# One fused attention-and-MLP kernel: partial products begun in PSUM by copies, weights split two operands at a time, activation differences on DVE, and four batches of attention first

## The chip, the core and the metric

The kernel runs on one core of one Trainium2 chip. Its time is the device time of one execution in microseconds (us): 1303.35 us before the change, the median of 3 runs (1302.53 to 1304.0). Engines: PE multiplies matrices into PSUM, DVE, ACT and POOL work on elements, SP issues the DMAs. Each engine takes its instructions strictly in the order of its own queue, so an instruction that waits holds up all that stand behind it.

## The reference

```python
B, H, S, D = 8, 12, 448, 64          # 3584 tokens, d_model 768, d_ff 2048
scores = q @ k.T / sqrt(D) - log(S)
attn = 1 / (1 + exp(-scores))        # a sigmoid, no softmax
x = heads_joined(attn @ v)           # (3584, 768)
h = x @ w_in                         # (3584, 2048)
g = h * clip(h + 3, 0, 6) / 6
out = g @ w_out                      # (3584, 768)
```

## The kernel before

**Seven products in place of eight.** Both matrix products of the MLP are cut into 2 x 2 blocks and computed with seven block products, `P1, P5, P6, P2, P7, P3, P4` in this order. Operands are sums and differences of blocks, and so are the results. Two batches together are one `n` (0 to 3).

**Each product in three passes.** An fp32 operand is split into a rounded high part and the rest (`split_w`: ACT casts, L263, DVE subtracts, L264), and PE multiplies high by high, high by low and low by high (`passes`). One product of one `j` is so 3 x 3 = 9 matmuls of 128x128 by 128x448.

**Stages.** The order of all work is written out: every step is put on a list by `at(place, ...)`, `place` being a planned time in us (`TS` for half a step of attention, `TU` for one product), and the list is sorted by it. PE, ACT, DVE and POOL keep this order. The DMAs on SP are put in order by the scheduler. `runs` sets the stages: attention for some batches, then the first MLP product for one `n`, and so on: A0 (batches 0, 1, 2), Q0, A1 (3, 4), Q1, A2 (5, 6), Q2, A3 (7), Q3, and at the end B, the second MLP product for all four `n`.

**Attention (A).** A step is one piece of scores for two heads on PE (`scores`), its sigmoid on ACT (L181), and, two steps later, the product with v on PE (`av`). There are 21 steps to a batch, each of two groups of 8 matmul instructions. `take` copies a finished bank out of PSUM (ACT, L209) and adds the second bank (DVE, L210). `t_ops` makes the block differences of x (POOL, L226) and splits them into the tiles `X` for PE (DVE, L217 and L218, 21 pairs per `n`). The `X` tiles of one `n` take the place of those of the `n` before.

**First MLP product (Q).** `quad(n, j)` for eight `j`: seven products, 63 matmuls. P1, P6, P7 and P4 accumulate on one PSUM bank (`za`), P5, P2 and P3 have banks of their own (`zb`). `keep` copies P1 and P5 to SBUF (ACT, L296), `add` forms the block results from PSUM and these copies (DVE, L301), `gate` applies the activation (ACT L314, DVE L315), `diffs` and `last` form the activation differences (POOL, L319 to L329), and SP stores all seven operands of the second product to DRAM. P6 must wait until P1 has been read, P7 until P1+P6 has been read, P4 until P1+P6+P7 has been read.

**Preparing the weights (prep).** The weights arrive as float64. For each of 16 pieces (`which`, `j`) and two halves `u`: ACT's `head` (L95), DVE's `body` and `tail` (L101, L102, L103, L111, L112; the high part in the tile `ab`, the low part in its second half), POOL's sum of both into the tile `wt` (L118), and after both halves four more sums on POOL (L125) and the store to DRAM (L127 one DMA for `which` 0, L130 seven for `which` 1). `wt` and `ab` have one buffer each, `st` (the loaded float64) two. The 8 pieces of `w_in` are prepared in A0 (five) and Q0 (three), those of `w_out` from Q1 on.

**Second MLP product (B).** `block(n)`: 56 units of 9 matmuls, operands loaded from DRAM, split by `split_2`.

## Time and profile before

| what | value |
|---|---|
| median of the runs shown | 1303.35 us |
| the profiled execution, its time | 1308.08 us |
| its span, first to last instruction | 1306.2 us |
| PE, DVE, ACT, POOL busy | 1153.3, 878.1, 649.4, 376.2 us |
| mean granted clock of PE | 0.946 |

The profiled execution took 4.73 us more than the median of the runs, and 1.88 us of its time lie outside its span. Stages overlap a little; the stage borders used below are those at which PE goes from one kind of matmul to the next. A busy share of the whole span says little here, since the stages have different limits: B runs with PE busy throughout, A and Q do not.

### The profile page before, as it was taken

What the parts mean: (1) busy time and instruction counts of PE and PEld (TensorE: products, weight loads), DVE (VectorE), ACT (ScalarE), POOL (GpSimd) and SP (SyncE); (2) the same over time, 40 slices, a digit from 0 to 9 for tenths busy, and PEclk for the clock granted to TensorE, in tenths of its full rate; (3) what the DMA queues carried; (4) which work ended last, traced back from release to release, by engine and by line L of the source; (5) the groups of instructions that cost most, each with busy time, mean ns of one, the idle gap of its engine ahead of it and who ended that gap; (6) DMA issues with size and microseconds to landing.
All of it is one profiled execution on the core that took longest, in us unless ns stands there. A gap on an engine that the chain in (4) does not pass through costs nothing. (4 is left out here: it accounts for less than half of the span.)

```text
span 1306.2 us, 18625 instructions
## 1 busy us (share of the span) xinstructions
PE 1153.3 (88%) x6720; PEld 904.8 (69%) x6720; DVE 878.1 (67%) x1352; ACT 649.4 (50%) x1150; POOL 376.2 (29%) x310
## 2 busy tenths in 40 slices
...
GB/s 248 299 162 192 217 264 229 206 204 136 156 237 212 236 236 218 142 220 213 198 219 192 79 238 245 199 170 266 263 164 159 145 155 155 114 179 187 114 139 59
DMA packets 81452, 250.26 MB, mean 192 GB/s; under 512 B 9040, under 2 KB 57552, under 8 KB 75856
## 3 DMA queue, kind: packets, MB, share of 16 engines
...
q10 hardware_dynamic: 144, 0.07, 0.0%
...
## 5 line engine op out<-in xcount | busy, mean ns | idle before, releaser
L288 PE MATMUL za<-x,w 128*128 128x448 f32 x1152 | 291.6, 407 | 106.2 <-DVE sn_c L301 48.4
L288 PEld LDWEIGHTS za<-x,w 128*128 128x128 f32 x1152 | 240.1, 212 | 146.7 <-issue 57.6
L397 PE MATMUL y<-x,w 128*128 128x448 f32 x1344 | 314.0, 368 | 0.0
L397 PEld LDWEIGHTS y<-x,w 128*128 128x128 f32 x1344 | 252.4, 188 | 25.4
L264 DVE TENSOR_TENSOR w<-raw,w 128x384 fp32r<-128x384 f32 x224 | 185.2, 837 | 43.8 <-ACT w L263 41.7
L181 ACT ACTIVATE a<-sc,bias_s 128x896 f32<-128x896 f32 x168 | 168.3, 1008 | 90.8 <-PE sc L170 45.4
L288 PE MATMUL zb<-x,w 128*128 128x448 f32 x864 | 196.2, 372 | 1.3 <-DVE x L217 1.1
L201 PE MATMUL pv<-a,v 64*64 64x448 f32 x1152 | 168.8, 561 | 28.1 <-DVE xr L210 23.5
L264 DVE TENSOR_TENSOR w<-w,w 128x384 fp32r<-128x384 f32 x224 | 126.4, 564 | 89.0 <-ACT w L263 88.4
L288 PEld LDWEIGHTS zb<-x,w 128*128 128x128 f32 x864 | 167.1, 194 | 17.3 <-DVE x L217 1.5
L263 ACT CAST w<-w 128x384 fp32r<-128x384 f32 x224 | 115.7, 517 | 126.9 <-PE yb L397 122.7
L397 PE MATMUL yb<-x,w 128*128 128x448 f32 x672 | 175.1, 368 | 0.0
L175 PE MATMUL sc<-qk 64*64 64x448 f32 x1152 | 160.7, 554 | 13.1 <-ACT a L181 7.7
L379 DVE TENSOR_TENSOR x<-gr,x 128x448 fp32r<-128x448 f32 x224 | 141.6, 632 | 7.6 <-ACT x L378 7.6
L118 POOL TENSOR_TENSOR wt<-ab 128x384 f32<-128x384 f32 x64 | 70.5, 1122 | 227.5 <-DVE ab L112 214.9
L397 PEld LDWEIGHTS yb<-x,w 128*128 128x128 f32 x672 | 126.2, 188 | 12.7
L378 ACT CAST x<-gr 128x448 fp32r<-128x448 f32 x224 | 127.2, 568 | 7.9 <-DMA gr<-gd 7.9
L263 ACT CAST w<-raw 128x384 fp32r<-128x384 f32 x224 | 110.7, 506 | 32.0 <-DMA raw<-wd 31.8
L201 PEld LDWEIGHTS pv<-a,v 64*64 64x64 f32 x1152 | 59.4, 138 | 92.7 <-issue 51.4
L175 PEld LDWEIGHTS sc<-qk 64*64 64x64 f32 x1152 | 56.3, 138 | 81.1 <-issue 49.4
L319 POOL TENSOR_TENSOR ga<-g,ga 128x448 f32<-128x448 f32 x32 | 42.6, 1332 | 229.5 <-DVE g L315 195.3
L314 ACT ACTIVATE ga<-sn_h,bias 128x448 f32<-128x448 f32 x32 | 21.4, 669 | 155.2 <-DMA gd<-ga 70.2
...
## 6 DMA issues: line engine op xcount, KB each, us to landing
...
```

The lines of the kernel that those rows point to most:

```text
L118: nc.gpsimd.tensor_tensor(out=o, in0=a[:, hs], in1=b[:, hs], op=ALU.add)
L175: nc.tensor.matmul(sc[halves[h], j, :S], k[halves[j], ks], q[halves[j]], start=True, stop=True)
L181: nc.scalar.activation(a, sc[:, :, :S], AF.Sigmoid, bias=bias_s, scale=scale)
L201: nc.tensor.matmul(pv[b, hp][h][halves[j], :S], v[halves[h], j * NC + c], a[halves[h], j], start=c == 0 and not (second and shared), stop= ...
L263: nc.scalar.copy(w[:, 0], src)
L264: nc.vector.tensor_tensor(out=w[:, 1], in0=src, in1=w[:, 0].bitcast(F32), op=ALU.subtract)
L288: nc.tensor.matmul(z[k][:, :S], w[:, wu, c * P : (c + 1) * P], X[n, k, c][:, xu], start=i == 0 and k in (P1, P5, P2, P3), stop=i == 3 * HC ...
L314: nc.scalar.activation(g[o], h, AF.Relu, bias=bias_3, scale=1.0)
L319: nc.gpsimd.tensor_tensor(out=a[:, 1], in0=g["g12"], in1=g["g11"], op=ALU.subtract)
L378: nc.scalar.copy(x[:, 0], src)
L379: nc.vector.tensor_tensor(out=x[:, 1], in0=src, in1=x[:, 0].bitcast(F32), op=ALU.subtract)
L397: nc.tensor.matmul(z[k][e][:, :S], w[:, wu, e * P : (e + 1) * P], x[:, xu], start=u == 0 and i == 0 and k in (P1, P5, P2, P3), stop=u == H ...
```

## The change

- **PSUM.** P2's bank is begun by a copy of P1 (`seed`, ACT) and P3's bank by P1+P6+P5 (`seed2`, DVE), and PE accumulates on top. The additions `h11` and `h12` fall away, and the gate reads the PSUM banks directly. `h22` stays.
- **Splits.** `split_w` splits two operands at once (128x768 in place of 128x384, four calls for seven products), `split_2` two units at once.
- **Differences.** The four activation differences of a quad go from POOL to DVE. `ga` gets a second buffer.
- **prep.** The tile `ab` is gone: `head` writes straight into `wt`, the body works there, the low part lies in the loaded tile `st` (elements 8 bytes apart), and POOL adds both with one instruction of 768. The planned places are closer: 8 pieces of `w_in` in A0, 15.2 apart; `w_out` three in Q0, three in Q1, two in A2.
- **Stages.** `runs` is (0,1,2,3), (4), (5,6), (7). The differences of x are formed in the tiles `xr` themselves (14 buffers), those of n = 1 at the start of A1.

```diff
-TS = 0.82
-TM = 0.2
+TS = 0.78
+TM = 0.207
...
         def head(u):
-            ab[u] = att.tile([P, 2, 2 * W], F32, tag="ab", name=f"ab_{which}_{j}_{u}")
-            nc.scalar.activation(ab[u][:, 0], st[u][:, :, 1].bitcast(F32), AF.Abs, bias=0.0, scale=2.0**-112)
+            if u == 0:
+                wt[0] = att.tile([P, NW + 1, W], F32, tag="wt", name=f"wt_{which}_{j}")
+            nc.scalar.activation(two(u), st[u][:, :, :, 1].bitcast(F32), AF.Abs, bias=0.0, scale=2.0**-112)
...
-            nc.vector.tensor_scalar(out=bi, in0=ai, scalar1=-(2**23), scalar2=None, op0=ALU.bitwise_and)
+            nc.vector.tensor_scalar(out=high, in0=ai, scalar1=-(2**23), scalar2=None, op0=ALU.bitwise_and)
             nc.vector.scalar_tensor_tensor(
-                out=b, in0=low.bitcast(U32), scalar=2.0**-52, in1=b, op0=ALU.mult, op1=ALU.mult
+                out=e, in0=low.bitcast(U32), scalar=2.0**-52, in1=e, op0=ALU.mult, op1=ALU.mult
             )
-            for h in range(2):
-                hs = slice(h * W, (h + 1) * W)
-                o = wt[0][:, ((P1, P2), (P4, NW))[u][h]]
-                nc.gpsimd.tensor_tensor(out=o, in0=a[:, hs], in1=b[:, hs], op=ALU.add)
+            nc.gpsimd.tensor_tensor(out=a, in0=a, in1=e, op=ALU.add)
...
+    pairs = ((P1, P5), (P6, P2), (P7, P3), (P4,))
+    def split_w(keys, src):
+        w = base.tile([P, 2, 2, W], F32R, tag="w", name=f"w_{'_'.join(map(str, keys[0]))}", bufs=4)
+        h, l = w[:, 0, : len(keys)], w[:, 1, : len(keys)]
+        nc.scalar.copy(h, src)
+        nc.vector.tensor_tensor(out=l, in0=src, in1=h.bitcast(F32), op=ALU.subtract)
...
+        def seed():
+            z[P2] = bank(f"zb_{n}_{j}_{P2}", bk[P2])
+            nc.scalar.copy(z[P2][:, :S], z[P1][:, :S])
+        def seed2():
+            z[P3] = bank(f"zb_{n}_{j}_{P3}", bk[P3])
+            nc.vector.tensor_tensor(out=z[P3][:, :S], in0=z[P1][:, :S], in1=sn["e"], op=ALU.add)
...
-            nc.gpsimd.tensor_tensor(out=a[:, 1], in0=g["g12"], in1=g["g11"], op=ALU.subtract)
-            nc.gpsimd.tensor_tensor(out=a[:, 2], in0=g["g22"], in1=a[:, 1], op=ALU.subtract)
+            nc.vector.tensor_tensor(out=a[:, 1], in0=g["g12"], in1=g["g11"], op=ALU.subtract)
+            nc.vector.tensor_tensor(out=a[:, 2], in0=g["g22"], in1=a[:, 1], op=ALU.subtract)
...
-    runs = [(0, 1, 2), (3, 4), (5, 6), (7,)]
+    runs = [(0, 1, 2, 3), (4,), (5, 6), (7,)]
...
+        if n == 1:
+            t_ops(n, range(HC), now + 1.0, 1.25)
...
-        prep(0, j, (14 + 20 * j) if j < 5 else marks[0] + 12.6 * (j - 5), 5)
-        prep(1, j, marks[1] + 5 + 30 * j, 9)
+        prep(0, j, 12 + 15.2 * j, 6)
```

The first place at which instructions move is the start of the second piece of weights in A0. Before, on ACT, its head (`ab_1_0`) waits for its load and for DVE and POOL to be done with the tile `ab`:

```order
L181 ACTIVATE a_2_3_393<-sc_2_3_388,bias_s 128x896 [waits PE_49,Activation_49]
L181 ACTIVATE a_2_4_404<-sc_2_4_399,bias_s 128x896 [waits PE_49,Activation_49]
L95 ACTIVATE ab_1_0_410<-st_1_0_342 128x768 [waits DMAHW7_49,DVE_49,Pool_49]
L181 ACTIVATE a_2_5_420<-sc_2_5_412,bias_s 128x896 [waits PE_49,Activation_49]
L209 COPY xr_2_437<-pv_2_0_378 128x448 [waits PE_49]
```

Before, on POOL, it is the first sum of this piece that also waits for a DMA (`DMAHW3`), the store of the piece before out of the one buffer of `wt`:

```order
L125 TENSOR_TENSOR wt_0_146<-wt_0_146 128x384 [waits Pool_49] x2
L125 TENSOR_TENSOR wt_0_146<-wt_0_146 128x384
L125 TENSOR_TENSOR wt_0_146<-wt_0_146 128x384 [waits Pool_49]
L118 TENSOR_TENSOR wt_1_341<-ab_1_0_410 128x384 [waits DMAHW3_49,DVE_49,Pool_49]
L118 TENSOR_TENSOR wt_1_341<-ab_1_0_410 128x384
```

Now, on ACT, from the second head of the first piece (`wt_0`) to the first head of the second (`wt_1`):

```order
L100 ACTIVATE wt_0_196<-st_0_1_189 128x768 [waits DMAHW3_49]
L180 ACTIVATE a_1_2_265<-sc_1_2_252,bias_s 128x896 [waits PE_49,Activation_49]
L180 ACTIVATE a_1_3_284<-sc_1_3_279,bias_s 128x896 [waits PE_49,Activation_49]
L180 ACTIVATE a_1_4_297<-sc_1_4_292,bias_s 128x896 [waits PE_49,Activation_49]
L180 ACTIVATE a_1_5_308<-sc_1_5_303,bias_s 128x896 [waits PE_49,Activation_49]
L208 COPY xr_1_321<-pv_1_0_267 128x448 [waits PE_49]
L180 ACTIVATE a_1_6_332<-sc_1_6_316,bias_s 128x896 [waits PE_49,Activation_49]
L180 ACTIVATE a_2_0_343<-sc_2_0_338,bias_s 128x896 [waits PE_49,Activation_49]
L100 ACTIVATE wt_1_356<-st_1_0_290 128x2x384 [waits DMAHW7_49,DMAHW3_49,Pool_49]
L180 ACTIVATE a_2_1_358<-sc_2_1_351,bias_s 128x896 [waits PE_49,Activation_49]
```

The head of the second piece now waits for two DMAs, its load (`DMAHW7`) and the store of `wt_0` (`DMAHW3`, on which SP's next load from that place, `raw_0_0<-wd_0`, waits too). All sigmoids behind it wait with it. Between the first heads of two pieces stand 10 sigmoids (9 once).

The second place is the second quad of Q0 on DVE. Before, with a half piece of weights (`ab_6_1`) in it:

```order
L301 TENSOR_TENSOR sn_1_c_1456<-za_1_1381,sn_1_1_1436 128x448
L101 TENSOR_SCALAR ab_6_1_1444<-ab_6_1_1444 128x768
L102 TENSOR_SCALAR ab_6_1_1444<-ab_6_1_1444 128x768
L103 SCALAR_TENSOR_TENSOR ab_6_1_1444<-st_6_1_1312,ab_6_1_1444 128x768
L264 TENSOR_TENSOR w_2_1_1461<-raw_2_0_1269,w_2_1_1461 128x384
L111 TENSOR_SCALAR ab_6_1_1444<-ab_6_1_1444 128x768
L112 SCALAR_TENSOR_TENSOR ab_6_1_1444<-st_6_1_1312,ab_6_1_1444 128x768
L301 TENSOR_TENSOR sn_1_h_1479<-zb_1_3_1446,sn_1_0_1420 128x448
L315 SCALAR_TENSOR_TENSOR ga_1_1481<-ga_1_1481,sn_1_h_1479 128x448
L264 TENSOR_TENSOR w_2_2_1484<-raw_2_0_1269,w_2_2_1484 128x384
L301 TENSOR_TENSOR sn_1_h_1497<-za_1_1381,sn_1_1_1436 128x448
```

Now, from `seed2` (L295) over a half piece (`wt_0`, L106 to L112), a double split (L253) and a gate (L316) to `h22` (L299), on which PE's P4 waits:

```order
L295 TENSOR_TENSOR zb_1_5_1734<-za_1_1668,sne_1_1714 128x448
L106 TENSOR_SCALAR wt_0_1636<-wt_0_1636 128x768
L107 TENSOR_SCALAR wt_0_1636<-wt_0_1636 128x768
L108 SCALAR_TENSOR_TENSOR wt_0_1636<-st_0_1_1648,wt_0_1636 128x768
L111 TENSOR_SCALAR st_0_1_1648<-wt_0_1636 128x768
L112 SCALAR_TENSOR_TENSOR st_0_1_1648<-st_0_1_1648 128x768
L253 TENSOR_TENSOR w_2_2_1753<-raw_2_1_1623,w_2_2_1753 128x768
L316 SCALAR_TENSOR_TENSOR ga_1_1751<-ga_1_1751,zb_1_3_1698 128x448
L299 TENSOR_TENSOR snh_1_1768<-za_1_1668,sne_1_1714 128x448
L316 SCALAR_TENSOR_TENSOR gc_1_1770<-gc_1_1770,snh_1_1768 128x448
```

Four additions of a quad have become two, seven splits four, and the five instructions of a half piece stand between `seed2` and `h22` in one block. The four differences (L320 to L326) follow at the end of the quad on DVE.

More of the change, by code (lines that the diff above doesn't have):

```diff
@@ L252, in tile_kernel @@
-    ring, rawt = {}, {}
-    def load_w1(n, j, part):
-        ks = (slice(0, 4), slice(4, NW))[part]
-        t = one.tile([P, ks.stop - ks.start, W], F32, tag=f"raw{part}", name=f"raw_{n}_{j}_{part}")
-        nc.sync.dma_start(out=t, in_=wd1[j][:, ks])
-        for i, k in enumerate(range(ks.start, ks.stop)):
-            rawt[n, j, k] = t[:, i]
-    def split_w(key, src):
-        w = base.tile([P, 2, W], F32R, tag="w", name=f"w_{'_'.join(map(str, key))}", bufs=8)
-        nc.scalar.copy(w[:, 0], src)
-        nc.vector.tensor_tensor(out=w[:, 1], in0=src, in1=w[:, 0].bitcast(F32), op=ALU.subtract)
-        ring[key] = w
@@ new lines, in tile_kernel, with load_w1 @@
+    ring, rawt = {}, {}
+    pairs = ((P1, P5), (P6, P2), (P7, P3), (P4,))
+    def load_w1(n, j, i):
+        ks = pairs[i]
+        t = one.tile([P, 2, W], F32, tag="raw", name=f"raw_{n}_{j}_{i}", bufs=4)
+        nc.sync.dma_start(out=t[:, : len(ks)], in_=wd1[j][:, ks[0] : ks[-1] + 1])
+        rawt[n, j, i] = t
+    def split_w(keys, src):
[3 more added lines that the diff above has]
+        nc.vector.tensor_tensor(out=l, in0=src, in1=h.bitcast(F32), op=ALU.subtract)
+        for i, key in enumerate(keys):
+            ring[key] = w[:, :, i]
@@ L347, in quad @@
-        at(place + 6 * TU + e + 0.1, gate, "g12", lambda: sn["h12"])
-        at(place + 6 * TU + e + 0.2, diffs)
-        at(place + 7 * TU + e, gate, "g21", lambda: z[P1][:, :S])
-        at(place + 7 * TU + e + 0.1, last)
+        for i, u in enumerate((2.2, 4.3, 6.3, 7.3)):
+            at(place + (u - 7) * TU, split_w1, n, j, i)
+            at(place + (u - 7) * TU - (12 if j else 9), load_w1, n, j, i)
+        at(place + 1 * TU + e, seed)
+        at(place + 2 * TU + e, keep)
+        at(place + 3 * TU + e, seed2)
@@ new lines, in quad @@
+        at(place + 4 * TU + e, gate, "g11")
+        at(place + 4.7 * TU + e, gate2, "g11")
+        at(place + 5 * TU + e, h22)
+        at(place + 5.4 * TU + e, gate, "g22")
+        at(place + 5.8 * TU + e, gate2, "g22")
+        at(place + 6 * TU + e, gate, "g12")
+        at(place + 6.5 * TU + e, gate2, "g12")
+        at(place + 7 * TU + e, gate, "g21")
+        at(place + 7.6 * TU + e, gate2, "g21")
+        at(place + 7.7 * TU + e, diffs)
+        at(place + 8.4 * TU + e, diffs2)
+        at(place + 4.7 * TU + 2, store, P1, lambda: g["g11"])
```

186 lines of the change are left out of this document (88 added, 98 removed).

## Prediction

> **What bounds the kernel now.** I first cut the span into its stages, A0, Q0, A1, Q1, A2, Q2, A3, Q3 and B (columns: stretch, length, busy time of PE, weight load, DVE, ACT and POOL with instruction counts, granted clock, DMA share, GB/s):
>
> ```profile
> span 1306.2 us, 18625 instructions
> 0.00:135.60 135.60, 107.13 (x1009) 48.07 (x1009) 85.14 (x114) 80.93 (x98) 55.08 (x55) 0.91 0.62 222
> 135.60:285.90 150.30, 117.07 (x509) 102.90 (x505) 108.62 (x145) 53.21 (x105) 69.11 (x56) 0.90 0.66 228
> 285.90:351.00 65.10, 64.37 (x673) 28.15 (x672) 39.01 (x60) 49.72 (x60) 19.65 (x16) 1.00 0.45 140
> 351.00:496.00 145.00, 118.01 (x512) 104.28 (x508) 110.99 (x151) 55.42 (x106) 67.99 (x54) 0.89 0.69 228
> 496.00:578.10 82.10, 70.79 (x673) 30.18 (x672) 61.38 (x82) 52.77 (x64) 37.89 (x32) 0.92 0.57 184
> 578.10:716.90 138.80, 114.83 (x510) 102.27 (x506) 96.82 (x138) 52.39 (x103) 62.99 (x50) 0.90 0.64 212
> 716.90:749.60 32.70, 32.01 (x338) 12.68 (x337) 20.06 (x30) 24.50 (x29) 14.56 (x12) 1.00 0.26 86
> 749.60:885.30 135.70, 112.36 (x508) 97.97 (x506) 96.40 (x146) 53.78 (x110) 43.20 (x32) 0.95 0.58 207
> 885.30:1302.00 416.70, 416.70 (x2017) 378.29 (x2015) 259.73 (x492) 225.80 (x477) 5.71 (x4) 1.00 0.43 162
> ```
>
> B is PE alone: 224 products in 416.7 us, 1.86 each. The quads have the same 224 products, 56 to a stage, so a Q stage could take 104.2; the four take 569.8 against 416.8. Of attention, two PE groups to a step:
>
> ```profile
> 28.33 0.93 PE L175 MATMUL sc<-qk 64*64 64x448 f32 x8
> 29.83 0.93 PE L170 MATMUL sc<-qk 64*64 64x448 f32 x8
> ```
>
> A step is 1.50, so 168 steps need 252; the A stages take 315. The excess, 153 in Q and 63 in A, is all there is to win. Next, the groups of instructions and the chain of waits say what PE lacks in Q, and the timeline of a quad of Q3 why:
>
> ```profile
> L288 PE MATMUL za<-x,w 128*128 128x448 f32 x1152 | 291.6, 407 | 106.2 <-DVE sn_c L301 48.4 <-DVE sn_h L301 47.6 <-ACT sn L296 6.1
> ACT ga L314 <- DMA gd<-ga: 70.2, 15, 6.2
> 814.52 2.41 DVE L264 TENSOR_TENSOR w<-raw,w 128x384 fp32r<-128x384 f32 x2
> 822.04 0.67 ACT L314 ACTIVATE ga<-sn_h,bias 128x448 f32<-128x448 f32 x1 [4.56 <-DMA gd<-ga]
> 829.02 2.41 DVE L264 TENSOR_TENSOR w<-raw,w 128x384 fp32r<-128x384 f32 x2
> ```
>
> The quad repeats every 14.5. ACT stands at the gate until the one buffer `ga` has been stored, the stores stand behind POOL's differences, DVE's gate stands behind ACT, and the additions that PE needs stand behind DVE's gate. In Q0 to Q2 POOL also prepares weights, and the quad takes 17.3 to 18.8.
>
> **The change, Q.** The second `ga` buffer and the differences on DVE cut this ring; 4.56 of ACT's wait goes. Next late is `h22`, on which P4 waits. DVE's work per quad, from these rows (mean ns of one):
>
> ```profile
> L264 DVE TENSOR_TENSOR w<-w,w 128x384 fp32r<-128x384 f32 x224 | 126.4, 564 | 89.0 <-ACT w L263 88.4
> L379 DVE TENSOR_TENSOR x<-gr,x 128x448 fp32r<-128x448 f32 x224 | 141.6, 632 | 7.6 <-ACT x L378 7.6
> L301 DVE TENSOR_TENSOR sn_h<-za,sn 128x448 f32<-128x448 f32 x32 | 19.8, 617 | 2.9 <-PE za L288 2.9
> L111 DVE TENSOR_SCALAR ab<-ab 128x768 int32<-128x768 int32 x32 | 17.8, 558 | 0.7
> L112 DVE SCALAR_TENSOR_TENSOR ab<-st,ab 128x768 f32<-128x768 uint32 x32 | 31.5, 984 | 1.1
> 91.36 0.55 DVE L101 TENSOR_SCALAR ab<-ab 128x768 f32<-128x768 f32 x1
> 95.01 0.62 DVE L210 TENSOR_TENSOR xr<-pv,xr 128x448 f32<-128x448 f32 x1
> ```
>
> 64 more elements cost 0.068, so a split of 768 costs 0.564 + 384 x 0.00106 = 0.97. Per quad: three of these and one of 0.56 (3.5), `seed2`, `h22` and four gates at 0.62 (3.7), four differences at 0.63 (2.5): 9.7 of 13.02. Before, seven splits (3.9), eight additions and gates (4.9) made 8.8 without contention. Q2 and Q3 have no preparation any more, hence no POOL work: PE is the bound, and for `h22` I add 0.3 a quad: Q2 = 107. Q3 adds the start, where PE waits for the last differences of x:
>
> ```profile
> 753.90 2.04 PE L288 MATMUL za<-x,w 128*128 128x448 f32 x5 [3.68 <-DVE w L264]
> 759.86 0.47 PE L288 MATMUL zb<-x,w 128*128 128x448 f32 x1 [1.13 <-DVE x L217]
> ```
>
> P6's operand is now sixth in the list instead of fifth; with these waits about as before, Q3 = 111.
>
> Q0 and Q1 keep three pieces each, six halves. A half took 3.65 of DVE (91.36 to 95.01). L111 now writes at 8-byte steps; its price lies between its own 0.56 and L112's 0.98, so a half is 3.65 to 4.1; I take 4.0 (both ends to the range). DVE: 8 x 9.7 + 6 x 4.0 = 102 of 104. Then contention: a subtraction on DVE alone, and beside POOL:
>
> ```profile
> 90.82 0.63 DVE L218 TENSOR_TENSOR x<-xt,x 128x448 fp32r<-128x448 f32 x1
> 97.69 1.32 DVE L217 CAST x<-xr 128x448 fp32r<-128x448 f32 x1
> 99.05 1.44 DVE L218 TENSOR_TENSOR x<-xr,x 128x448 fp32r<-128x448 f32 x1
> 25.16 1.95 POOL L118 TENSOR_TENSOR wt<-ab 128x384 f32<-128x384 f32 x2 [4.79 <-DVE ab L112]
> 27.20 3.99 POOL L125 TENSOR_TENSOR wt<-wt 128x384 f32<-128x384 f32 x4
> ```
>
> POOL's work in a stage is 3 x (1.95 + 1.95 + 3.99) = 24, during which DVE runs at about half speed: 12 more, 114. And a block of 4.0 right behind `seed2` delays `h22`, and PE, by about 2, six times. These overlap; I take DVE's 114, plus 8 of such waits, plus 5 for the half clock after waits (below): 127 each, between 112 (all hidden) and 150 (nothing gained). The skill speaks against the differences on DVE: the Trainium skill, "SBUF — State Buffer", § SBUF: two separate sides, says that a DVE operation with two SBUF inputs and a GpSimd operation exclude each other for a whole instruction. The trace agrees (0.63 against 1.44); by that rule all 24 come on top, DVE is at 126 and the stage nearer 140.
>
> `seed` puts an ACT copy between P1 and P6, where `keep` (same size) stood; P5's 1.86 covers it, and without that cover it costs about 0.6 a quad, 19 in all.
>
> **The change, A0.** It gets 84 steps (126) and eight pieces of weights. The first piece of before shows the chain of one piece:
>
> ```profile
> 13.61 0.93 ACT L95 ACTIVATE ab<-st 128x768 f32<-128x768 f32 x1
> 20.40 0.91 ACT L95 ACTIVATE ab<-st 128x768 f32<-128x768 f32 x1 [1.09 <-POOL wt L118]
> 31.22 0.33 SPq L127 DMA_DIRECT2D wd<-wt  x1
> 35.87 0.80 SPq L257 DMA_DIRECT2D raw<-wd  x2
> ```
>
> First head at 13.61, second head, its half on DVE, POOL's two sums at 25.16 and four at 27.20 (rows above), the store at 31.22; the load of the stored piece starts when it has landed, 35.87. That is 22.3. Before, only POOL waited for the landing. Now the next piece's head does, in ACT's queue, with every sigmoid behind it; PE has scores for two steps in PSUM and then stops. Ten sigmoids, 15.0, separate the heads, so each piece makes PE wait about 7. After a wait PE is slow at first:
>
> ```profile
> 43.51 1.16 PE L201 MATMUL pv<-a,v 64*64 64x448 f32 x8 [3.72 <-DMA v<-vP]
> 44.43 1.97 PE L170 MATMUL sc<-qk 64*64 64x448 f32 x8
> 45.92 1.89 PE L201 MATMUL pv<-a,v 64*64 64x448 f32 x8
> 90.54 1.02 PE L201 MATMUL pv<-a,v 64*64 64x448 f32 x3 [7.12 <-DVE xr L210]
> ```
>
> Groups come every 1.49 instead of 0.75 (44.43 to 45.92), for some 3 us: the second head, four sigmoids on, comes 1.5 later. A piece is 22.3 + 1.5 + 0.2 (L111) = 24.0. In two or three of the periods, up to seven splits of x (1.0 alone; 97.69 and 99.05 make 2.8 beside POOL) and as many POOL differences stand ahead of the second half or of POOL's sums: nothing to 21, I take 14. First head: one sigmoid (1.5) and one copy (0.5) earlier than 13.61, 11.6. After the last first head, ten sigmoids and two steps of lag, 18. A0 = 11.6 + 7 x 24.0 + 14 + 18 = 212. The takes that cost 7.12 before (90.54) now fit into these waits.
>
> **The other stages.** A1: 21 steps (31.6), but 21 splits of x (21 to 58) and DVE's takes behind them: 36. A2: 42 steps (63), two pieces 12 to 13 steps apart whose chain ends in seven stores, a wait of about 8, puts and half clock 9: 80. A3 33. B: ACT and DVE have half of PE's time free (259.73 of 416.70), double splits are a little cheaper: 416.7. End 4.2 (1306.2 less 1302.0).
>
> Sum: 212 + 127 + 36 + 127 + 80 + 107 + 33 + 111 + 416.7 + 4.2 = 1253.9, against 1306.2 of the profiled span. Its time was 1.9 longer than its span and 4.7 above the median of the runs: 1253.9 + 1.9 - 4.7 = 1251.
>
> **Rivals.** *The chain is hidden* (ACT's wait short, the store landing early). Then A0 is bound by PE and by DVE around batch 1, where 21 splits of x at 1.0 to 2.8 (40), six takes (4) and four halves (16) make 60 in 33 us of PE: 126 + 4 + 27 = 157, and the time is 54 lower (212 - 157), 1197. For it: before, POOL's wait on this store was rare; against: the wait in the order of ACT, and 22.3 against 15.0. Chance 0.17.
>
> *Q0 and Q1 gain nothing*, because DVE and POOL exclude each other and DVE's queue sets the pace: as before, 150.3 + 145.0, that is 41 more, 1292. The rule on SBUF named above points this way. For it: 108.62 and 110.99 of DVE busy there now; against: ACT's wait for `ga` is gone. Chance 0.13.
>
> *Slower: elements 8 bytes apart cost double* in what writes them or adds them. L111 and L112 then take about 1.9 each, a half 2.3 more, POOL's sum 1.95 more. Each piece's chain in A0 grows by 4.2 (30), Q0 and Q1 by 6 x (2.3 + 1) = 20 each, A2 by 8: 78 more, 1329. It decides from two thirds of that on (52 more is the time before). Against it: L112 reads such elements at 0.98, no more than a plain operation of 768; no row shows a write. The Trainium skill, "VectorE: DVE Perf Modes", § What auto-detection actually checks, asks for no dense step of an fp32 operand; no run here shows it. Chance 0.07. The rest, 0.05, is a DMA queue or a tile's slot that holds up SP or ACT longer than seen.
>
> **How the numbers follow.** The forecast, 1251, has 0.58; its own unknowns (Q0 and Q1 -15 to +23 each, A0 -14 to +10, A1 to +15) seldom add up: 1215 to 1290. The range 1190 to 1300 holds nearly all of that, two thirds of the hidden chain and most of "Q gains nothing". 0.2% (2.6 us) is about what a measurement of this kernel can tell from no change. Faster: 0.58 + 0.17 + 0.10 of 0.13 + 0.01 = 0.86; the same 0.03; slower 0.11.
>
> **What would show it.** Right: in A0, ACT's first head of each piece after the first waits on the DMA `wd<-wt` about 7 us, PE idles at a sigmoid seven times, and the heads are 23 to 28 apart; ACT never waits for `ga`; Q2 within 105 to 110; Q0 and Q1 longer than Q2 by 10 to 30, with PE waiting for `snh` and `zb` behind blocks of L106 to L112; B unchanged. Wrong: A0 under 165, Q0 at 145 or more, L111 or L112 over 1.3, or B with PE idle.

## The result, and the profile after

The changed kernel takes 1286.87 us, median of 4 runs (1286.2 to 1288.0), against 1303.67 of the kernel before (4 runs, 1302.53 to 1307.59; the 1303.35 above is of three): ratio 0.9867, 95% interval 0.9845 to 0.9889. It is 17 us or 1.3% faster, a third of the 52 us that were forecast. The profiled execution took 1288.0, its span is 1286.2 (before: 1308.08 and 1306.2).

The stage table of after, with the columns of the one of before (stretch, length, busy time of PE, weight load, DVE, ACT, POOL with counts, granted clock, DMA share, GB/s):

```profile
span 1286.2 us, 17828 instructions
0.00:215.50 215.50, 155.04 (x1344) 55.69 (x1344) 117.88 (x148) 109.09 (x128) 78.92 (x65) 0.83 0.57 200
215.50:356.60 141.10, 114.56 (x512) 101.50 (x508) 103.16 (x138) 51.84 (x83) 31.46 (x20) 0.90 0.72 245
356.60:393.10 36.50, 33.43 (x338) 14.11 (x337) 35.50 (x53) 25.84 (x30) 15.64 (x12) 1.00 0.40 127
393.10:528.60 135.50, 113.78 (x511) 101.09 (x508) 101.83 (x137) 51.52 (x83) 29.17 (x18) 0.90 0.72 239
528.60:613.30 84.70, 72.72 (x674) 29.90 (x673) 63.44 (x81) 52.07 (x61) 32.82 (x24) 0.94 0.50 162
613.30:716.50 103.20, 103.20 (x510) 94.02 (x508) 66.91 (x106) 46.56 (x77) 0.00 (x0) 1.00 0.70 223
716.50:748.90 32.40, 31.93 (x338) 12.60 (x337) 21.73 (x33) 24.60 (x28) 10.15 (x8) 1.00 0.25 80
748.90:873.40 124.50, 110.02 (x509) 97.59 (x506) 85.07 (x131) 51.74 (x84) 5.39 (x5) 0.95 0.65 225
873.40:1282.00 408.60, 408.60 (x2017) 378.31 (x2015) 243.61 (x275) 199.34 (x256) 0.00 (x0) 1.00 0.46 165
```

| stage | before | forecast | after | after less forecast |
|---|---|---|---|---|
| A0 | 135.6 | 212 | 215.5 | +3.5 |
| Q0 | 150.3 | 127 | 141.1 | +14.1 |
| A1 | 65.1 | 36 | 36.5 | +0.5 |
| Q1 | 145.0 | 127 | 135.5 | +8.5 |
| A2 | 82.1 | 80 | 84.7 | +4.7 |
| Q2 | 138.8 | 107 | 103.2 | -3.8 |
| A3 | 32.7 | 33 | 32.4 | -0.6 |
| Q3 | 135.7 | 111 | 124.5 | +13.5 |
| B | 416.7 | 416.7 | 408.6 | -8.1 |

The A stages grew by 53.6, the Q stages shrank by 65.5, B by 8.1: 20.0 between the two spans. The miss lies in Q0, Q1 and Q3, 36 us together; A0 came as forecast.

**A0.** ACT's first heads of the second and third piece, in the timeline of after:

```profile
36.11 0.89 ACT L100 ACTIVATE wt<-st 128x768 f32<-128x768 f32 x1 [7.77 <-DMA wd<-wt]
60.50 0.89 ACT L100 ACTIVATE wt<-st 128x768 f32<-128x768 f32 x1 [6.97 <-DMA wd<-wt]
```

and PE behind them:

```profile
37.95 1.77 PE L169 MATMUL sc<-qk 64*64 64x448 f32 x8 [6.99 <-ACT a L180]
62.34 1.77 PE L174 MATMUL sc<-qk 64*64 64x448 f32 x8 [6.22 <-ACT a L180]
```

ACT stands about 7 us at the store of the piece before, these heads are 24.4 apart, and PE idles at a sigmoid, seven times in A0: the forecast chain. Later, from 75 to 140, where DVE also splits x, three heads are 27 to 31 apart and ACT stands 10 to 15.

**Q0.** A quad late in the stage. First DVE in the timeline of after, from a half piece (L106 to L112) to `seed2` (L295), then POOL, then PE:

```profile
322.91 0.55 DVE L106 TENSOR_SCALAR wt<-wt 128x768 f32<-128x768 f32 x1
...
325.09 0.56 DVE L111 TENSOR_SCALAR st<-wt 128x768 int32<-128x768 int32 x1
325.68 0.96 DVE L112 SCALAR_TENSOR_TENSOR st<-st 128x768 f32<-128x768 uint32 x1
326.56 0.61 DVE L316 SCALAR_TENSOR_TENSOR g<-g,za 128x448 f32<-128x448 f32 x1
327.09 1.98 DVE L320 TENSOR_TENSOR ga<-g,ga 128x448 f32<-128x448 f32 x1
329.11 1.31 DVE L321 TENSOR_TENSOR ga<-gc,ga 128x448 f32<-128x448 f32 x1
330.34 1.41 DVE L324 TENSOR_TENSOR gc<-gc,g 128x448 f32<-128x448 f32 x1
331.67 1.41 DVE L326 TENSOR_TENSOR gt<-g,ga 128x448 f32<-128x448 f32 x1
333.00 1.74 DVE L253 TENSOR_TENSOR w<-raw,w 128x768 fp32r<-128x768 f32 x1
334.67 0.62 DVE L295 TENSOR_TENSOR zb<-za,sne 128x448 f32<-128x448 f32 x1
```

```profile
326.72 1.87 POOL L115 TENSOR_TENSOR wt<-wt,st 128x768 f32<-128x768 f32 x1 [11.37 <-DVE st L112]
328.67 5.26 POOL L122 TENSOR_TENSOR wt<-wt 128x384 f32<-128x384 f32 x4
```

```profile
326.55 2.02 PE L279 MATMUL zb<-x,w 128*128 128x448 f32 x9
335.35 3.73 PE L279 MATMUL za<-x,w 128*128 128x448 f32 x9 [6.78 <-DVE zb L295]
```

PE has finished P6 and then P2 (at 328.57); P7 goes into the bank that `seed2` has yet to read, and `seed2`, 0.62 long, starts at 334.67. Ahead of it DVE does a half piece, a gate, four differences and a split; just then POOL makes the sums for which that half was the last input, and the five operations from 327.09 to 334.74 take 7.6 in place of 3.4 (4 x 0.62 + 0.96). PE loses 6.78. The list of waits of the whole run has PE waiting for `zb` (L295) 15 times, 47.6 us, and for `snh`, which I had expected to be as frequent, 3 times, 8.9, of which 7.2 is a wait in Q3 with another cause (below):

```profile
PE za L279 <- DVE zb L295: 47.6, 15, 6.8
PE za L279 <- DVE snh L299: 8.9, 3, 7.2
```

ACT's waits for the stores of `ga` are gone; L111, now writing at 8-byte steps, takes 0.56 and L112 0.96, as before.

**B.** The same matmuls have another pace (page of before, then of after: busy, mean ns of one, idle):

```profile
L397 PE MATMUL y<-x,w 128*128 128x448 f32 x1344 | 314.0, 368 | 0.0
```

```profile
L404 PE MATMUL y<-x,w 128*128 128x448 f32 x1344 | 308.8, 365 | 0.0
```

From start to start a matmul takes 206.67 ns in B of before and 202.67 in B of after, all through the stage. I take it for no part of the change: in the table below, kernels whose B is the same code as in after have 408.7 or 416.8.

### The profile page after: what moved, and what is told of

It is laid out like the page before. It is cut to its first block, busy times and chain, and to the rows that moved or that the text cites. A ratio compares the mean times of both kernels' runs of the same rounds, so it can differ in the third digit from the quotient of the medians.

```text
span 1286.2 us, 17828 instructions
## 1 busy us (share of the span) xinstructions
PE 1143.3 (89%) x6720; PEld 884.8 (69%) x6720; DVE 839.1 (65%) x1096; ACT 613.5 (48%) x830; POOL 203.5 (16%) x150
## 4 chain that ended last, share of the span: by engine, by line
PE 48%; DVE 5%; DMA 2%; issue 1%; POOL 1%; ACT 1%; ACTq 0%; DVEq 0%; POOLq 0%
PE y L404 21%; PE yb L404 11%; PE za L279 8%; PE zb L279 6%; DVE x L217 2%; DMA raw<-wd 1%; DVE x L216 1%; PE sc L174 1%; PE pv L200 1%; DVE w L253 1%; DVE xr L209 0%; POOL wt L122 0%; DMA wd<-wt 0%; POOL xr L221 0%; ACT w L252 0%
## 5 line engine op out<-in xcount | busy, mean ns | idle before, releaser
L279 PE MATMUL za<-x,w 128*128 128x448 f32 x1152 | 273.4, 388 | 60.1 <-DVE zb L295 47.6
L253 DVE TENSOR_TENSOR w<-w,w 128x768 fp32r<-128x768 f32 x112 | 107.3, 958 | 152.2 <-ACT w L252 150.8
L252 ACT CAST w<-w 128x768 fp32r<-128x768 f32 x112 | 93.6, 836 | 191.4 <-PE yb L404 183.8
L253 DVE TENSOR_TENSOR w<-raw,w 128x768 fp32r<-128x768 f32 (+1 forms) x128 | 125.6, 982 | 90.0 <-ACT w L252 82.5
L279 PEld LDWEIGHTS zb<-x,w 128*128 128x128 f32 x864 | 166.8, 193 | 17.9 <-DVE x L216 2.1
L387 DVE TENSOR_TENSOR x<-gr,x 128x896 fp32r<-128x896 f32 x112 | 121.4, 1084 | 5.6 <-ACT x L386 5.6
L115 POOL TENSOR_TENSOR wt<-wt,st 128x768 f32<-128x768 f32 x32 | 62.5, 1954 | 366.8 <-DVE st L112 347.3
L386 ACT CAST x<-gr 128x896 fp32r<-128x896 f32 x112 | 105.3, 940 | 5.6 <-DMA gr<-gd 5.6
L252 ACT CAST w<-raw 128x768 fp32r<-128x768 f32 (+1 forms) x128 | 95.5, 748 | 13.5 <-DMA raw<-wd 13.5
L221 POOL TENSOR_TENSOR xr<-xr,xr 128x448 f32<-128x448 f32 x48 | 63.1, 1319 | 188.7 <-DVE x L217 186.5
L217 DVE TENSOR_TENSOR x<-xr,x 128x448 fp32r<-128x448 f32 x84 | 87.3, 1039 | 2.9
```

The costliest lines, as they stand in the source:

```text
L115: nc.gpsimd.tensor_tensor(out=a, in0=a, in1=e, op=ALU.add)
L217: nc.vector.tensor_tensor(out=x[:, 1], in0=xr[q], in1=x[:, 0].bitcast(F32), op=ALU.subtract)
L221: nc.gpsimd.tensor_tensor(out=xr[o], in0=xr[x], in1=xr[y], op=ALU.subtract)
L252: nc.scalar.copy(h, src)
L253: nc.vector.tensor_tensor(out=l, in0=src, in1=h.bitcast(F32), op=ALU.subtract)
L279: nc.tensor.matmul(z[k][:, :S], w[:, wu, c * P : (c + 1) * P], X[n, k, c][:, xu], start=i == 0 and k in (P1, P5), stop=i == 3 * HC - 1, sk ...
```

## The experiments

Sixteen kernels, each the changed kernel with the edits named below. The stages are from their traces. The runs were on several chips, on which the kernel before took 1302 to 1309; so each ratio is to the kernel before on the same chip, and medians of different rows compare to a few us only:

| kernel | median us | ratio, 95% interval | A0 | Q0 | Q1 | A2 | Q2 | Q3 | B |
|---|---|---|---|---|---|---|---|---|---|
| the change | 1286.9 | 0.987, 0.985-0.989 | 215.5 | 141.1 | 135.5 | 84.7 | 103.2 | 124.5 | 408.6 |
| ab2 | 1249.9 | 0.956, 0.950-0.962 | 174.2 | 137.8 | 134.3 | 83.0 | 103.3 | 125.3 | 416.8 |
| nohalf | 1222.0 | 0.934, 0.928-0.941 | 214.2 | 116.7 | 108.1 | 72.4 | 103.6 | 125.5 | 408.7 |
| poolsmall | 1248.8 | 0.956, 0.951-0.961 | 215.2 | 127.7 | 120.7 | 73.3 | 103.4 | 125.1 | 408.7 |
| noprep | 1203.8 | 0.923, 0.919-0.927 | 214.6 | 110.5 | 103.3 | 64.1 | 103.3 | 122.6 | 408.7 |
| diffspool | 1285.2 | 0.983, 0.977-0.990 | 214.3 | 132.9 | 132.2 | 84.9 | 103.4 | 124.5 | 408.7 |
| spread | 1262.6 | 0.968, 0.963-0.973 | 213.5 | 130.2 | 121.0 | 88.2 | 103.5 | 124.0 | 408.7 |
| spread_poolsmall | 1228.0 | 0.942, 0.937-0.947 | 213.1 | 117.6 | 110.1 | 73.1 | 103.3 | 123.4 | 408.7 |
| addsplit | 1282.8 | 0.985, 0.980-0.990 | 215.3 | 138.4 | 134.1 | 84.7 | 103.3 | 125.0 | 416.8 |
| w2act | 1281.0 | 0.981, 0.979-0.984 | 215.6 | 139.1 | 135.6 | 84.9 | 103.3 | 118.5 | 408.7 |
| ga1 | 1301.9 | 0.998, 0.995-1.001 | 213.4 | 143.8 | 141.0 | 84.8 | 103.3 | 131.7 | 416.8 |
| ga1pool | 1310.9 | 1.004, 1.001-1.007 | 214.3 | 147.9 | 140.4 | 84.7 | 104.2 | 132.2 | 416.8 |
| noseed | 1314.7 | 1.006, 1.003-1.009 | 215.0 | 147.9 | 143.5 | 85.1 | 109.0 | 128.8 | 408.7 |
| noseed_ring | 1333.3 | 1.021, 1.017-1.026 | 215.4 | 152.1 | 146.0 | 84.9 | 111.8 | 137.8 | 408.7 |
| single_ring | 1309.8 | 1.003, 1.000-1.006 | 215.1 | 145.7 | 145.4 | 84.8 | 104.2 | 131.7 | 408.7 |
| combo1 | 1214.3 | 0.930, 0.927-0.933 | 172.3 | 120.4 | 117.1 | 83.1 | 117.1 | 119.2 | 408.7 |
| combo2 | 1213.6 | 0.933, 0.928-0.938 | 170.4 | 122.4 | 116.9 | 85.1 | 116.4 | 118.9 | 408.7 |

My theory at the start: A0 loses to ACT's wait for the store; Q0 and Q1 to blocks of halves in front of `seed2` and to POOL's locks on DVE. The rivals were DVE's backlog in A0 and the sheer sum of DVE's work, or late raw weights, in Q.

### A0: ab2

```diff
-            if u == 0:
-                wt[0] = att.tile([P, NW + 1, W], F32, tag="wt", name=f"wt_{which}_{j}")
-            nc.scalar.activation(two(u), st[u][:, :, :, 1].bitcast(F32), AF.Abs, bias=0.0, scale=2.0**-112)
+            ab[u] = att.tile([P, 2, W], F32, tag="ab", name=f"ab_{which}_{j}_{u}", bufs=2)
+            nc.scalar.activation(ab[u], st[u][:, :, :, 1].bitcast(F32), AF.Abs, bias=0.0, scale=2.0**-112)
...
-            nc.gpsimd.tensor_tensor(out=a, in0=a, in1=e, op=ALU.add)
+            if u == 0:
+                wt[0] = att.tile([P, NW + 1, W], F32, tag="wt", name=f"wt_{which}_{j}")
+            nc.gpsimd.tensor_tensor(out=two(u), in0=a, in1=e, op=ALU.add)
```

> The changed kernel, with a two-buffer tile of its own for the absolute values and their halves (head and body); `wt` is taken and written first by POOL's addition, so that POOL and no longer ACT waits for the store of the piece before. Nothing of the computation changes. Theory, ACT's wait for the store sets A0 (heads 24 apart instead of 15): A0 falls from 215.5 to 155-170, A2 by 3-8, the Q stages keep their times within 4, the time is 1230-1243. Rival, the chain of a piece only hides another limit, DVE's work around batch 1 (splits of x, halves and takes): A0 stays over 190 and the time over 1262. Rival, POOL's wait is as bad, because DVE's halves and POOL's differences of x queue up behind it: A0 over 175 with PE waiting for `xr` and `x`.

A0 ends at 174.2 in place of 215.5, 41 less; in ab2's list of waits POOL now stands at the store, and PE's matmuls have no wait for ACT's sigmoids:

```profile
POOL wt L118 <- DMA wd<-wt: 31.9, 5, 8.6
```

The median falls by 37, with B at the slower pace in its profile. So the theory holds for A0 in its cause: the price of `head` writing straight into the one buffer of `wt` is 41. The sizes missed: A0 is 4 over the expected range, A2 fell by 2 and not by 3 to 8, and the median is 7 over, about what B's pace is worth. Of the 48 still over PE's 126, 20.8 are waits of PE for DVE's takes, five of 3 to 5 us; the takes stand behind splits of x, four of them behind a half as well. The longest:

```profile
111.39 1.02 PE L203 MATMUL pv<-a,v 64*64 64x448 f32 x3 [5.32 <-DVE xr L212]
```

### Q0 and Q1, halves and POOL: nohalf, poolsmall, noprep

These three kernels leave out part of the preparation of w_out, so that their second weight has other values; only their times are read. nohalf ends `body` for w_out with POOL's addition, ahead of the five DVE instructions. poolsmall lets POOL's additions for w_out do 8 of 384 columns, leaves out the four sums, and stores other slots of the same size:

```diff
-            nc.gpsimd.tensor_tensor(out=a, in0=a, in1=e, op=ALU.add)
+            n = W if which == 0 else 8
+            nc.gpsimd.tensor_tensor(out=a[:, :, :n], in0=a[:, :, :n], in1=e[:, :, :n], op=ALU.add)
...
-                nc.gpsimd.tensor_tensor(out=w[:, o], in0=w[:, x], in1=w[:, y], op=op)
+                if which == 0:
+                    nc.gpsimd.tensor_tensor(out=w[:, o], in0=w[:, x], in1=w[:, y], op=op)
...
-                    nc.sync.dma_start(out=wd2[k][:, j], in_=w[:, k])
+                    nc.sync.dma_start(out=wd2[k][:, j], in_=w[:, (P1, P2, P4, NW)[k % 4]])
```

noprep has both edits, except that the addition which ends its `body` also does 8 columns only.

> The changed kernel without the five DVE instructions that form the halves of w_out (second weight): the heads, POOL's additions and sums, the stores and all else stay, so the second weight's values are wrong and the time alone is read. It takes about 24 us of DVE out of Q0 and of Q1 and 8 out of A2. Theory, a block of halves in front of `seed2` and `h22`, plus DVE's load, makes Q0 and Q1 long: both fall from 141 and 135.5 to 112-118, A2 from 84.7 to 76-80, the time to 1230-1243. Rival, the exclusion between DVE and POOL is what costs, and POOL's work is still there: Q0 and Q1 at 122-130, time 1255-1270. Rival, late loads of raw weights: Q0 and Q1 stay at 130 or more with ACT waiting for `raw`, time 1275 or more.

> The changed kernel with POOL's two additions per piece of w_out on 8 columns instead of 384, and without its four sums; the stores send other slots of the same size, so the second weight's values are wrong and the time alone is read. It takes 24 us of POOL out of Q0 and of Q1; DVE's instructions are all there. Theory, POOL holds DVE up for whole instructions (24 us a stage): Q0 and Q1 fall to 115-122, the time to 1240-1255. Rival, the blocks of halves in DVE's queue cost by themselves: Q0 and Q1 fall by 8 or less each, the time is over 1268. A2 falls by 0-6 under both.

> The changed kernel with w_out's preparation almost without DVE and POOL: none of the five DVE instructions of a half, POOL's additions on 8 columns and no sums; heads, loads and seven stores per piece stay (of other slots), so the second weight's values are wrong and the time alone is read. Alone, the halves gone were worth 24.5 and 27 us in Q0 and Q1, POOL's work gone 13.5 and 15. Theory, these two are all of the excess over Q2 and they add: Q0 and Q1 at 103-108 each, the time 1200-1212. Rival, they overlap, since both are the same time in which DVE and POOL exclude each other, and a third cause (late raw weights behind the stores, the heads in ACT's queue) holds the rest: Q0 and Q1 at 110-116, time 1213 or more.

Q0 and Q1 of poolsmall, then Q0, Q1 and A2 of noprep, in the columns of the stage table:

```profile
215.20:342.80 127.60, 111.72 (x511) 99.53 (x508) 88.03 (x138) 51.61 (x83) 5.64 (x8) 0.93 0.79 272
379.40:500.00 120.60, 107.91 (x507) 96.47 (x504) 87.51 (x137) 51.38 (x83) 2.86 (x6) 0.97 0.80 268
```

```profile
214.60:325.00 110.40, 105.51 (x510) 95.34 (x506) 67.83 (x108) 51.37 (x83) 4.37 (x8) 0.98 0.90 315
361.60:464.80 103.20, 103.20 (x507) 94.01 (x504) 67.07 (x107) 51.09 (x83) 1.67 (x6) 1.00 0.91 313
464.80:528.80 64.00, 63.53 (x673) 25.47 (x672) 39.82 (x61) 51.97 (x61) 16.56 (x16) 1.00 0.66 213
```

Without w_out's preparation Q1 is at PE's bound, 103.3, and A2 at 64.1, its 42 steps. So the preparation is all of the excess in Q1 (32.2) and in A2 (20.6), and 30.6 of the 38 in Q0. The other 7 of Q0 are its start, below. The shares overlap: in Q1, 27.4 without the halves and 14.8 without POOL's work make 42.2, the two together 32.2; 10 belong to both, which I read as the time in which one waits for the other. The theory's "they add" fell; both rivals that made one of the two the only cause fell as well. Sizes missed here too: without halves Q1, A2 and the median (by 8) came out under the expected ranges, and without POOL's work Q0 stayed 6 over its range and A2 fell by 11, not by 6 at most. DVE's busy time in Q0 tells the size of the lock: 103.2 with POOL's work, 88.0 without; 15 of the 103 were waiting that the profile counts as busy.

At the start of Q0 (not tried further) ACT's row in the timeline of after shows a raw weight that is not there:

```profile
225.48 0.83 ACT L252 CAST w<-raw 128x768 fp32r<-128x768 f32 x1 [5.49 <-DMA raw<-wd]
```

The first weight's last piece is stored only at 218.38, and SP issues this load behind that store, at 218.79; it lands at 225.46.

### Q0 and Q1, where the work stands: spread, spread_poolsmall, addsplit, diffspool

spread calls the five DVE instructions of a half of w_out one by one:

```diff
-            at(place + u * gap + 0.9, body, u)
+                for i in range(5):
+                    at(place + u * gap + 0.9 + 1.6 * i, part, u, i)
+                at(place + u * gap + 0.9 + 1.6 * 4, add, u)
```

spread_poolsmall has poolsmall's edit as well. addsplit makes POOL's addition two instructions of 384 columns. diffspool puts `nc.gpsimd` for `nc.vector` in `diffs` and `diffs2`.

> The changed kernel with the five DVE instructions of a half of w_out apart, 1.6 us of planned time between them, instead of one after the other; the same instructions, and nothing of the computation changes. Theory, a block in front of `seed2` is what PE waits for, and removing the blocks took 24.5 and 27 us from Q0 and Q1 for that reason: with at most one of the five in front, PE's waits for `zb` in Q0 to Q1 fall from 48 to under 25, Q0 and Q1 to 120-130, the time to 1258-1275. Rival, the sheer amount of DVE work bounds the two stages: Q0 and Q1 stay within 4 of 141 and 135.5, the time within 8 of 1287. Rival, the halves end later, POOL's sums and the stores with them, and ACT's next head waits longer: Q0 and Q1 grow, time over 1295.

> The changed kernel with the halves of w_out apart (1.6 us of planned time between the five instructions) and POOL's additions for w_out on 8 columns, without its sums (the second weight's values are wrong, the time alone is read). All DVE work is there, in no block, and POOL's locks are gone. Theory, blocks and locks are the two losses, and 102 us of DVE work fits beside 104 of PE: Q0 and Q1 fall to 105-112, the time to 1218-1238. Rival, DVE's queue is full at 102 of 104, so that each wait for PE is lost for good: Q0 and Q1 at 115-121, the time 1238 or more.

> The changed kernel with POOL's addition of 768 columns as two of 384, for both weights. Nothing of the computation changes. POOL's work is the same length, but no single instruction is over 1.4. Theory, a DVE operation beside POOL waits until POOL's instruction ends: the longest splits (2.2-2.6 for 0.96) go to 2.0 or less, Q0 and Q1 fall by 1-5 each, the time by 2-10. Rival, only POOL's total counts: DVE's mean times and the two stages stay within 1.5.

> The changed kernel with the four activation differences of a quad on POOL again, as before the change, with two buffers of `ga` kept. Nothing of the computation changes. It takes 2.5 us a quad off DVE and puts about 4 on POOL. Theory, DVE and POOL exclude each other in Q0 and Q1, so it hardly matters which of them does the work there: Q0 and Q1 change by less than 6 each, Q2 stays at 103-105 because PE is its bound, the time is within 10 of 1287. Rival, the sheer length of DVE's queue makes Q0 and Q1 long: both fall by 12-18, the time to 1252-1265. Rival, POOL's differences come so late that the stores hold up `gc` and the next gates: Q0 to Q3 grow by 5-15 each, time 1300 or more.

The same DVE instructions, only apart, are worth 10.9 in Q0 and 14.5 in Q1, and the median 24: blocks in front of `seed2` are a cause, the sum of DVE's work is not. (PE's waits for `zb` in the two stages fell from 46 to 28, a little less than expected.) With POOL's work gone too, Q1 is 110.1 with all the halves on DVE (85.6 busy): both causes together, and DVE's queue is not full. Q0, at 117.6, is 6 over the range, its start of 7 being still there. (A2 got 3.5 longer under spread: the spread halves end later, ACT's head of the second piece waits 12.2 for the store in place of 9.9, and PE 10.5 at a sigmoid in place of 4.6.) addsplit cuts the longest split in Q0 and Q1 from 2.63 to 1.80 and shortens the two stages by 2.7 and 1.4: as expected in direction, but its median, 4 under the change's, says little with B's pace 8 apart, so this stays weak. diffspool moves the two stages by -8 and -3, not the 12 to 18 of the rival that has DVE's length as the cause; its median is 2 lower, its profiled execution, the shortest of four, 11. That the differences went to DVE is not the gain; whether it costs some us in Q0 is not settled.

### What made a quad shorter: ga1, ga1pool, noseed, noseed_ring, single_ring

ga1 has one buffer of `ga`; ga1pool also diffspool's edit. noseed undoes the seeds:

```diff
-            z[P2] = bank(f"zb_{n}_{j}_{P2}", bk[P2])
-            nc.scalar.copy(z[P2][:, :S], z[P1][:, :S])
+            sn["p"] = one.tile([P, S], F32, tag="snp", name=f"snp_{n}_{j}")
+            nc.scalar.copy(sn["p"], z[P1][:, :S])
...
+        def plus(k, t):
+            nc.vector.tensor_tensor(out=sn[t], in0=z[k][:, :S], in1=sn[t], op=ALU.add)
```

noseed_ring is noseed with ga1pool's edits, so that of the quad's edits only the double splits are left; in single_ring only the seeds are left (one operand to a split, one buffer, POOL's differences).

> The changed kernel with one buffer of `ga`, as before the change; the differences stay on DVE. Nothing of the computation changes. Theory, the second buffer is what cut the ring of store, gate and additions: ACT waits again for `ga` to be stored, Q2 rises from 103.2 to 115-140, Q0 and Q1 by 0-10 each, the time to 1310 or more. Rival, on DVE the differences end so early that the store has landed before the next gate (planned 5 us ahead of it): Q2 stays at 103-106 and the time within 8 of 1287.

> The changed kernel with one buffer of `ga` and the four differences on POOL: both parts of the change that touch the ring undone, with the seeds, the double splits and the order of the batches kept. Nothing of the computation changes. Theory, the ring of before is closed again: ACT waits for `ga` some 3-5 a quad, Q2 is 125-140, Q3 130-145, the time 1325-1360. Rival, the seeds alone cut the ring, since DVE's additions no longer stand between PE and the gates: Q2 stays at 103-110, the time within 12 of 1287.

> The changed kernel with the seeds undone: P2's and P3's sums start empty, P1's product and P1+P5 are kept in SBUF, and DVE adds each finished product to the kept one ahead of its gate, two more DVE operations (0.62 each) a quad; the second buffer of `ga`, the differences on DVE and the double splits stay. Nothing of the computation changes. Last call's runs left Q2 at 103-104 with one buffer and with the differences on POOL, so neither is what shortened a quad. Theory, the seeds did: with DVE's additions again between PE's product and ACT's gate, Q2 rises from 103.2 to 112-125, Q0 and Q1 by 5-15 each, the time to 1305-1340. Rival, the second buffer or the moved differences are enough without the seeds: Q2 103-106, Q0 and Q1 plus 0-6, the time 1285-1300.

> The changed kernel with the seeds undone, one buffer of `ga` and the differences on POOL: of the quad's edits only the double splits are left, with the order of the batches and of the preparation. Nothing of the computation changes. Theory, with no seed, no second buffer and POOL's differences the ring of before is closed whatever the splits: quads of 14.3-14.7 in Q2 and Q3, Q2 at 114-119, ACT waiting 3-5 a quad for `ga`, the time 1325-1365. Rival, it was the double splits (1.0 us less a quad on DVE and on ACT each) that freed the quad: Q2 stays at 103-107.

> The changed kernel with the weights of a quad split one operand at a time (seven ACT copies and seven DVE subtractions of 384 instead of four and four), one buffer of `ga` and the differences on POOL: of the quad's edits only the seeds are left. Nothing of the computation changes. Theory, the seeds alone cut the ring: Q2 103-107, Q3 within 5 of the 132 that it had with the double splits, the time 1308-1325. Rival, seeds and double splits are both needed: Q2 112-119, ACT waiting for `ga` or DVE's queue full, time 1330 or more.

Q2, where nothing disturbs the quads, separates them: 103.3, 104.2, 109.0, 111.8 and 104.2. ACT's gate of `g11` in Q2 of noseed_ring, in its timeline, and the addition and gate on DVE that come around it:

```profile
701.66 0.67 ACT L316 ACTIVATE ga<-snp,bias 128x448 f32<-128x448 f32 x1 [3.46 <-POOL gt L329]
...
715.65 0.67 ACT L316 ACTIVATE ga<-snp,bias 128x448 f32<-128x448 f32 x1 [3.44 <-POOL gt L329]
```

```profile
703.96 0.62 DVE L319 SCALAR_TENSOR_TENSOR ga<-ga,snp 128x448 f32<-128x448 f32 x1
704.50 0.62 DVE L302 TENSOR_TENSOR snh<-za,sne 128x448 f32<-128x448 f32 x1
```

and the same gate in ga1pool, with seeds, one buffer and POOL's differences:

```profile
684.28 0.64 ACT L313 ACTIVATE ga<-zb,bias 128x448 f32<-128x448 f32 x1 [2.50 <-PE zb L279]
697.22 0.63 ACT L313 ACTIVATE ga<-zb,bias 128x448 f32<-128x448 f32 x1 [2.43 <-PE zb L279]
```

Without the seeds a ring like that of before is closed, 14.0 a quad: ACT waits 3.4 until POOL's last difference has read `ga` (before, until `ga` was stored), `h22` (L302) stands behind that gate's second half on DVE, PE's P4 behind `h22`. With the seeds ACT waits for PE, and a quad takes 12.9. So in Q2 the seeds cut the ring (111.8 to 104.2), and not what I had named, the second buffer and the differences on DVE; these two without the seeds give 109.0. Two additions of 0.62, which stood between PE's end and ACT's gate, are out of the ring with the seeds. I had counted the seeds only as DVE time. The double splits are worth nothing that the time shows: 1309.8 without them in single_ring, 1310.9 with them in ga1pool. In ga1 and ga1pool the rival was right on Q2, but the medians came out 7 and 12 over what it allowed, for the second buffer has another use. In noseed and noseed_ring Q2 rose 3 and 2 less than their ranges say.

Where other waits push the quads, ga1 loses 2.7, 5.5 and 7.2 in Q0, Q1 and Q3. All of the quad's edits but the splits together are worth 46 (1333.3 to 1286.9). The rest of the change (splits, preparation, order of the batches), seen from there, costs: noseed_ring is 2.1% slower than the kernel before.

### Q3: w2act

```diff
-        nc.sync.dma_start(out=t, in_=wd2[k])
+        (nc.scalar if k < 2 else nc.sync).dma_start(out=t, in_=wd2[k])
```

> The changed kernel with the loads of the first two slots of the second weight (`w2_0`, `w2_1`, 1.5 MB each) issued from ACT's queue, at their planned place 24 and 9 us ahead of the last stage's products, instead of from SyncE's, which issues them at 766 and 768, 107 us early; all else stays. Theory, these two loads hold up the raw weights of quads 1 and 2 of Q3 (ACT's wait of 7.19 for `raw`, PE's of 7.15 behind it): the wait goes, Q3 falls from 124.5 to 116-118, the time to 1277-1281. Rival, the raw loads are late because SyncE stands at the stores of `ga` and `gc` before them: Q3 stays within 2 of 124.5. Rival, `w2_0` comes late now: PE waits at the start of the last stage, which grows by 3-10. No other stage changes by more than 4.

In after, SP issues the two loads at 766 and 768; ACT and PE then stand in the second quad:

```profile
788.18 0.83 ACT L252 CAST w<-raw 128x768 fp32r<-128x768 f32 x1 [7.19 <-DMA raw<-wd]
```

```profile
791.12 5.61 PE L279 MATMUL za<-x,w 128*128 128x448 f32 x18 [7.15 <-DVE snh L299]
```

With the loads issued at 838 and 853 the wait is gone, Q3 is 118.5 (6.0 less, 116 to 118 expected), and the median is 6 lower. The theory holds: the two loads held up the raw weights. The edit moves them to another queue and to a later time at once, so which of the two is needed is not shown. B starts without delay.

### A version to beat both: combo1, combo2

combo1 joins ab2, spread (in the Q stages) and w2act, and lays two pieces of w_out each in Q0, Q1 and Q2; combo2 spreads the halves in A0 and A2 too.

```diff
-    for j, place in enumerate([marks[0] + 10 + 30 * i for i in range(3)] + [marks[1] + 10 + 30 * i for i in range(3)] + [starts[2] + 5, starts[2] + 25]):
-        prep(1, j, place, 8)
+    for j, place in enumerate([marks[i // 2] + 10 + 45 * (i % 2) for i in range(6)] + [starts[2] + 5, starts[2] + 25]):
+        prep(1, j, place, 8, j < 6)
```

> The changed kernel with four things together: the tile of its own for the heads (POOL waits for the store instead of ACT), the halves of w_out apart in the quad stages, `w2_0` and `w2_1` loaded from ACT's queue, and the six pieces of w_out that lay three each in Q0 and Q1 now two each in Q0, Q1 and Q2. Nothing of the computation changes. Theory, the losses are separate and add: A0 170, Q0 118-126, A1 37, Q1 110-117, A2 83, Q2 104-112, A3 33, Q3 118, last stage 409 or 417: time 1190-1212. Rival, they overlap (with A0 shorter, stores and loads of the first weight fall later and the raw weights of Q0 with them; Q2 takes what Q0 and Q1 give): time 1220-1240.

> The combination of the last call (1214.3) with the halves apart in the attention stages too, 1.1 us of planned time between the five instructions for the first weight in A0, 1.6 for the second in A2. Nothing of the computation changes. Theory, in A0 and A2 PE waits for DVE's takes of attention's result (22 us in A0, 11 in A2) because each stands behind a block of halves: A0 falls from 168.6 to 152-162, A2 from 83.1 to 74-80, the time to 1193-1208. Rival, DVE's work around batch 1 is too much wherever it stands, or the later ends of the halves hold up POOL and the store: A0 and A2 stay within 4, time 1208-1220.

combo1 takes 1214.3, 7.0% less than before and 5.6% less than the change. The losses were separate in the main, though the median is 2 over the expected range and Q1 and Q2 are 117.1 each where 110 to 117 and 104 to 112 were expected: two pieces still cost 14 a stage. combo2 is the same within its interval; A0 and A2 moved by -2 and +2, so the rival holds: DVE's work around batch 1 is too much wherever it stands, or the later ends of the halves take back what is won. These two were not told apart.

## Why the prediction was right or wrong

- **A0, 212 forecast, 215.5 measured: right**, with its mechanism (heads 24 apart, ACT's 7 at the store, PE idle at sigmoids); ab2 shows it by its removal. Its sum holds term by term: 13.2 for 11.6 up to the first head, 184.4 for 182 from there to the last, 17.9 for 18 behind it. Two takes still cost PE 8.0, which were to fit into the other waits. The rival "the chain is hidden" fell.
- **A1, A2, A3**: 36.5, 84.7 and 32.4 for 36, 80 and 33. A2's two pieces cost 20.6.
- **Q2, 107 forecast, 103.2 measured: right in size, wrong in its cause.** The step "the second `ga` buffer and the differences on DVE cut this ring" failed; the seeds cut it. The 0.3 a quad for `h22` was nothing, and the faster pace of the matmuls (below) gave the rest.
- **Q0 and Q1, 127 forecast, 141.1 and 135.5 measured: this is the step that failed**, "I take DVE's 114, plus 8 of such waits, plus 5". Its DVE part was too high: the quads of a stage keep DVE busy for 67.8 (noprep) and not 78, the six halves for 20.2 (between poolsmall and noprep) and not 24, POOL's lock for 15 and not 12; 103 and not 114. (I had added the durations of a quad, 9.7. Records that follow each other overlap by up to 0.1, so that a quad of Q2 has 8.9 busy, and the last quad's differences fall behind the stage.) But DVE's sum is not what sets the stage. DVE is idle for 38 of the 141, 14.8 of them for ACT's casts and 11.1 for PE's products, and both wait for DVE in turn; a quad has no slack (12.9 of PE), so what stands in front of `seed2` at the wrong time adds to the stage. Seen from PE, over the 103 of Q2: waits of 26.5 in Q0 and 21.7 in Q1, nearly all for `seed2`, and 11.4 and 10.6 more of busy time in slow matmuls behind them, for which I had put 5. The preparation cost 31 to 32, for which I had put 23 over PE's 104. The 7 at the start of Q0 I had not looked for at all.
- **The rival "DVE and POOL exclude each other", 1292, was nearer than the forecast** in time, and in part right in its mechanism. In the two stages it was no nearer: it had 295 for both, the forecast 254, and 277 were measured; its nearness in time comes from the other stages, Q3 above all. The rule that I weighed, of the Trainium skill, "SBUF — State Buffer", § SBUF: two separate sides, is exclusion for a whole instruction. The trace agrees in kind: five DVE operations took 7.6 for 3.4 beside POOL's. In size, POOL's work cost the stages 13.4 and 14.8, not the 24 on top that I had worked out from it; that the stage then came out at its 140 is in part chance, since the halves cost more by their place.
- **Q3, 111 forecast, 124.5 measured.** 6.0 are the two large loads, which the scheduler put ahead of raw weights; I had taken SP's queue as it was. The rest is in w2act too (118.5 against PE's 103): waits of 8.3 in all, 5.2 of them for `w` and `x` at the start, and slow products after them. I had put 4 for it all over Q2.
- **B, no change forecast: 8.1 less**, which I take for the pace of the matmuls and not for the change (last section). Without it the profiled spans would differ by 12.
- **L111 and L112 at 8-byte steps**: 0.56 and 0.96; the slower rival fell.
- **Two slips that change nothing**: 212 - 157 is 55 and not 54, and DVE was busy for 62% of B before, not for half.

The sum of the stages' misses is 32.3, which is 1286.2 less 1253.9.

What stays open: how much of Q0's start the late store of the first weight makes, what the 14 for two spread pieces in Q1 of combo1 are made of, and what sets the pace of B.
